# Other unread products in the norms, and new ones in front of gate and up pieces

## The chip, the core and the metric

The kernel runs on one core of a Trainium2 chip. The metric is the device time in microseconds (us) of one execution. Five engines share the core: TensorE (PE in the profile; its weight loads are PEld) multiplies, VectorE (DVE) and ScalarE (ACT) do elementwise work and copies, GpSimd (POOL) does nothing here after four fills, and SyncE (SP) issues the loads. Sixteen DMA engines move the data from HBM into the on-chip store (SBUF). PE writes its results into PSUM, in banks of 512 fp32 columns by 128 partitions.

## The reference

Four rows of 640 numbers go through attention, a gated MLP, the same attention and the same MLP again, in fp32 throughout:

```python
x = x + A(layernorm(x))      # q = x @ wq; softmax(q k / sqrt(128)) v per head; @ wo
x = x + B(layernorm(x))      # relu(x @ W_gate) * (x @ W_up) @ W_down
x = x + A(layernorm(x))
x = x + B(layernorm(x))
```

Attention has 32 heads of 128 and looks at the last 1024 of 4096 cached keys and values, for each of the 4 batch rows. Keys, values and `wq`/`wo` are used in both layers, and so are `W_gate`, `W_up` (640 x 1728) and `W_down` (1728 x 640). The layer norm has no weights.

## The kernel before

All large operands lie in HBM as rows by partition, in the order of their use: `heads` (queries' weights, keys, values and output weights of the groups of four heads), `kept` (the same for the last 5 heads, groups K0 with three and K1 with two, which stay on chip from layer 0 to layer 1) and `mlp`. They stream through one tile, `store`, of 50,624 fp32 columns. `plan` (L116 to L198) lists every load: which columns of which row go to which place. `load` (L203) issues from the front of that list on SyncE's queue for as long as the place of the next load is free, and `done` (L245) marks columns as free after the last product that reads them, and calls `load`. The tile framework then makes SyncE wait for that product. So the loads keep the order of the plan, and a load whose place is still being read holds back everything behind it. In most of the run the pieces have up to 16,320 columns (8 MB). In layer 0's MLP the kept groups hold most of the store, and gate, up and down weights pass in pieces of 640 to 1344 columns through what is left; layer 1's first pieces of `heads` (L173 to L189) then go to places that layer 0's MLP and layer 1's work on the kept groups free one by one.

The order of instructions is the order in which the program is written; nothing rearranges it. A layer is `attention(layer)` (L484) and `forward(layer)` (L532). `normalized` (L337) opens both: VectorE sums `y` (L342), ScalarE copies it (L343), PE turns the partition sums into means by products with a selecting matrix (`mean`, L330, products at L334), VectorE subtracts the mean (L346), ScalarE squares and sums (L348), PE transposes the centred rows (L352 and L354) and VectorE copies them out as `xT` (L356), the stationary operand of all that follows. `deviation` gives the scale. In `attention`, `query` makes q of one group from `xT` (products through `product`, L242, into banks `m`), `query_turned` (L401) transposes it, `scores` multiplies with keys into `ps` (layer 1's first group: into `pp`), `softmax`, `turned` (L430), `values` into `po` and `project` into `y` follow. In `forward`, `gate(j)` (L536) makes a slice of gate and up: `gate(3)` the smaller rest first, then 0, 1 and 2. Each has 5 row chunks c by 4 column groups g (3 groups for the rest), each a product of 256 moving columns (128 for the rest) with 32 stationary ones, four side by side in the array by `tile_position`. `gated`, `hidden` and `down` finish the MLP.

A product whose result nobody reads is called an unread product here. The kernel has two helpers for them: `busy(n)` (L314) makes n transposes of the 128 x 128 identity into `po`, `fill(n)` (L321) n products of the identity with itself. Both only act while `waits[0]` is set. `normalized` sets it, `forward` sets it to `layer == 0` after `gate(3)`, and `values` to `layer == 0` at a layer's last group. In the norm, `busy(2)` stands between the sum and the mean (L344), and `fill(1)` between the squares and the transposes (L349).

The names of profile rows: L242 is `product`, so weights of all kinds go by the tile they write; L318 is `busy`, L325 is `fill`, L211 is the issue of a load. One fp32 product shows as two MATMULs, a transpose as one.

Of the kernel before, what the change touches and what calls it, by code (L numbers as in the profile page):

```python
# [13 lines left out]
P = 128  # L14
# [81 lines left out]
def decode_kernel(ctx: ExitStack, tc: tile.TileContext, x, source, sel, out):  # L96
    nc = tc.nc
# [42 lines left out]
    def near(c, row="heads"):  # L140

        return max(x for x in ROWS[row][2] if x <= c)
# [22 lines left out]
    lo = 0  # L165
# [6 lines left out]
    lo = HELD  # L172
# [9 lines left out]
    for n in 4096, 6144, 9728:  # L182
        hi = near(lo + n)
        to = put(1, "heads", to, lo, hi)
        lo = hi
    hi = near(lo + 4608)
    to = put(1, "heads", to, lo, hi)
    lo, hi = hi, near(hi + STORE - to)
# [12 lines left out]
    held = {}  # L201
# [18 lines left out]
    def place(layer, row, lo):  # L220

        if row == "heads" and lo < HELD:
            return first_q, lo, HELD - lo
        most = KV
        if row == "kept" and layer:
            if AHEAD[0] <= lo < AHEAD[1]:
                return probs, QUARTER + lo - AHEAD[0], AHEAD[1] - lo
            if BACK[0] <= lo < BACK[1]:
                return store, HOME + lo - BACK[0], BACK[1] - lo
            most = min(x - lo for x in (AHEAD[0], BACK[0], FRONT) if x > lo)  # L230
        for first, m, p in held[key(layer, row)]:
            if first <= lo < first + m:
                return store, p + lo - first, min(first + m - lo, most)
        raise KeyError((layer, row, lo))

    def product(out, by, layer, row, lo, n, start, stop, rows=slice(0, P), **how):

        a = 0
        while a < n:
            t, p, m = place(layer, row, lo + a)  # L240
            z = min(n, a + m)
            nc.tensor.matmul(out[:, a:z], by, t[rows, p:p + z - a], start=start and not a, stop=stop and z == n, **how)  # L242
            a = z

    def done(layer, row, lo, n):  # L245

        if row == "kept" and layer == 0:
            return
        if row == "kept":
            for p in range(lo, lo + n):  # L250
                if BACK[0] <= p < BACK[1]:
                    live[HOME + p - BACK[0]] = False
                elif not (AHEAD[0] <= p < AHEAD[1] or HOME <= p < HOME + BACK[1] - BACK[0]):
                    live[p] = False
        else:
            for first, m, p in held[key(layer, row)]:
                a, b = max(lo, first) - first, min(lo + n, first + m) - first
                if a < b:
                    live[p + a:p + b] = [False] * (b - a)
        load()  # L260
# [12 lines left out]
    sel_sb = const.tile([P, P + 32], F32, name="sel_sb")  # L273
# [14 lines left out]
    pp = ps_p.tile([P, 2, 512], F32, name="pp")  # L288
# [6 lines left out]
    def bank(n):  # L295

        turn_of[0] ^= 1
        return banks[turn_of[0]][:, :n]
# [4 lines left out]
    ident, sel_q = sel_sb[:, :P], sel_sb[:, P:]  # L303
# [6 lines left out]
    for g in range(4):  # L310
        nc.tensor.matmul(y[32 * g:32 * g + B], ident[:B, :B], probs[:B, g * QUARTER:(g + 1) * QUARTER],
                         start=True, stop=True, tile_position=(0, 32 * g))

    def busy(n):  # L314

        if waits[0]:
            for _ in range(n):
                nc.tensor.transpose(po[:, :P], ident, ident)  # L318


    def fill(n, to=po):  # L321

        if waits[0]:
            for _ in range(n):
                nc.tensor.matmul(to[:, :P], ident, ident, start=True, stop=True)  # L325


    waits = [False]

    def mean(a):  # L330

        m = bank(1)
        for g in range(4):
            nc.tensor.matmul(m[32 * g:32 * g + 32], sel_q, a, start=True, stop=True, tile_position=(0, 32 * g))  # L334
        return m

    def normalized():  # L337

        ysb, xc, sq = probs[:, :QUARTER], gates[:, :QUARTER], gates[:, QUARTER:2 * QUARTER]
        waits[0] = True  # L340
        su = small.tile([P, 1], F32, name="su", bufs=1)
        nc.vector.tensor_reduce(su, y, axis=AX.X, op=ALU.add)  # L342
        nc.scalar.copy(ysb, y)  # L343
        busy(2)  # L344
        mu = mean(su)
        nc.vector.tensor_tensor(xc, ysb, mu.to_broadcast([P, QUARTER]), op=ALU.subtract)  # L346
        ss = small.tile([P, 1], F32, name="ss", bufs=1)
        nc.scalar.activation(sq, xc, AF.Square, accum_out=ss)  # L348
        fill(1)  # L349

        pt = pp[:, 0, :KC * 32].rearrange("p (c x) -> p c x", c=KC)
        nc.tensor.transpose(pt[:, :4], xc[:, :P], ident)  # L352
        for g in range(4):
            nc.tensor.matmul(pt[32 * g:32 * g + 32, 4, :B], xc[:, P:], ident[:, 32 * g:32 * g + B],  # L354
                             start=True, stop=True, tile_position=(0, 32 * g))
        nc.vector.tensor_copy(xT[:, :KC * B].rearrange("p (c b) -> p c b", b=B), pt[:, :, :B])  # L356
        return ss
# [13 lines left out]
    def go_on():  # L371

        nc.tensor.matmul(y, ident, probs[:, :QUARTER], start=True, stop=False)
# [157 lines left out]

    def forward(layer):  # L532
        ss = normalized()
        gus, hTs = {}, {}

        def gate(j):  # L536
            n, groups = (P, 4) if j < 3 else (64, 3)
            at = GU0 + j * GU if j < 3 else 0
            gus[j] = pp[:, j % 2, :2 * P]
            for c in range(KC):  # L540
                for g in range(groups):
                    lo = at + (c * groups + g) * 2 * n
                    product(gus[j][32 * g:32 * g + 32], xT[:, B * c:B * c + 32], layer, "mlp", lo, 2 * n,
                            start=c == 0, stop=c == KC - 1, tile_position=(0, 32 * g))
                    done(layer, "mlp", lo, 2 * n)

        def gated(j):
            n, p = (P, P) if j < 3 else (64, 96)
            gu = gus.pop(j)
            at = 256 * (j % 2)  # L550
            a, b = gates[:p, at:at + n], gates[:p, at + P:at + P + n]
            nc.scalar.activation(a, gu[:p, :n], AF.Relu, scale=rstd[:p])
            nc.vector.scalar_tensor_tensor(b, gu[:p, n:2 * n], rstd[:p], a, op0=ALU.mult, op1=ALU.mult)
            return b

        def hidden(j, h):
            hTs[j] = small.tile([P, 4, B], F32, name="hT", bufs=4)
            ph = bank(P).rearrange("p (f x) -> p f x", f=4)
            if j < 3:
                nc.tensor.transpose(ph, h, ident)  # L560
                nc.vector.tensor_copy(hTs[j], ph[:, :, :B])
                return

            for g, lo, f in (0, 0, 0), (1, 64, 0), (2, 0, 1), (2, 64, 1):
                nc.tensor.matmul(ph[lo:lo + 64, f, :B], h, ident[:96, 32 * g:32 * g + B],
                                 start=True, stop=True, tile_position=(0, lo))
            nc.vector.tensor_copy(hTs[j][:, :2], ph[:, :2, :B])

        def down(j, last=False):
            for f in range(4 if j < 3 else 1):  # L570
                lo = WD1 + j * WD + f * D if j < 3 else WD0
                for g in range(4):
                    product(y[32 * g:32 * g + B], hTs[j][:, f], layer, "mlp", lo + g * QUARTER, QUARTER,
                            start=False, stop=last and f == 3, tile_position=(0, 32 * g))
                done(layer, "mlp", lo, D)
                if j == 3:
                    fill(1)
                elif not (last and f > 1):
                    busy(1)
                if j == 0 and f == 1:  # L580
                    fill(2)
            if j == 3:
                for g in range(4):
                    r = slice(64 * (g // 2), 64 * (g // 2) + 64)
                    product(y[32 * g:32 * g + B], hTs[j][r, 1], layer, "mlp", TAIL + g % 2 * QUARTER, QUARTER,
                            start=False, stop=False, rows=r, tile_position=(r.start, 32 * g))
                done(layer, "mlp", TAIL, 2 * QUARTER)

        gate(3)
        waits[0] = layer == 0  # L590
        rstd = deviation(ss)
        go_on()
        fill(1)
        h = gated(3)
        for j, j1 in (3, 0), (0, 1), (1, 2):
            gate(j1)
            hidden(j, h)
            fill(1)
            h = gated(j1)
        down(3)  # L600
        down(0)
        hidden(2, h)
        if layer == 0:
            nc.scalar.copy(away[:, :512].rearrange("p (j n) -> p j n", j=2), pp[:, :, 256:])
            for i in range(2):
                nc.scalar.copy(away[:, 512 + 384 * i:896 + 384 * i], banks[i][:, P:])
            live[AWAY[0]:AWAY[1]] = [True] * 1280
        down(1)
        down(2, last=True)
# [64 lines left out]
```

## Time and profile before

| | |
|---|---|
| time, median of 3 runs | 731.74 us (731.72 to 732.07) |
| profiled execution, its own time | 734.14 us |
| its span, first to last instruction | 732.4 us |
| mean granted clock of PE | 0.816 |
| busy: PE, PEld, DVE, ACT | 445.4, 158.6, 75.2, 54.2 us |
| bytes read from HBM | 310.57 MB, mean 424 GB/s over the span |

The profiled execution has its own time, 734.14 us, beside the median of the unprofiled ones, and its span leaves out what lies before the first and after the last instruction. PE's busy time is the time in which at least one product is under way, not a measure of how much it does. The granted clock is the share of full speed that the chip gave PE. "DMA share" in a window is the mean over the 16 DMA engines of the time in which they have packets under way, and can come out slightly above 1 in short windows.

### The profile page before, as it was taken

What the parts mean: (1) busy time and instruction counts of PE and PEld (TensorE: products, weight loads), DVE (VectorE), ACT (ScalarE), POOL (GpSimd) and SP (SyncE); (2) the same over time, 40 slices, a digit from 0 to 9 for tenths busy, and PEclk for the clock granted to TensorE, in tenths of its full rate; (3) what the DMA queues carried; (4) which work ended last, traced back from release to release, by engine and by line L of the source; (5) the groups of instructions that cost most, each with busy time, mean ns of one, the idle gap of its engine ahead of it and who ended that gap; (6) DMA issues with size and microseconds to landing.
All of it is one profiled execution on the core that took longest, in us unless ns stands there. A gap on an engine that the chain in (4) does not pass through costs nothing.

```text
span 732.4 us, 8422 instructions
## 1 busy us (share of the span) xinstructions
PE 445.4 (61%) x3844; PEld 158.6 (22%) x3844; DVE 75.2 (10%) x279; ACT 54.2 (7%) x101; POOL 0.2 (0%) x4
## 2 busy tenths in 40 slices
PE   0845565655655554619879896365656555556576
PEld 0211112222112121103344241021121112112123
DVE  1111001010010101002101211001010010101011
ACT  0200000000000000001302210000000000000100
POOL 0000000000000000000000000000000000000000
PEclk9888887776777777759999999677787878778989
DMA  9999999999999999999999999999999999999996
GB/s 405 445 405 438 440 445 416 434 431 444 441 419 428 419 441 448 419 431 425 419 392 407 392 427 455 423 441 434 433 427 444 424 441 426 438 437 420 423 429 286
DMA packets 13291, 311.19 MB, mean 425 GB/s; under 512 B 1476, under 2 KB 1732, under 8 KB 6984
## 3 DMA queue, kind: packets, MB, share of 16 engines
q1 hardware_dynamic: 13104, 310.56, 98.9%
q8 instruction: 30, 0.49, 0.2%
q10 hardware_dynamic: 152, 0.09, 0.0%
q14 instruction: 5, 0.04, 0.0%
HBM read 310.57 MB, written 0.08 MB: 424 GB/s over the span
## 4 chain that ended last, share of the span: by engine, by line
DMA 73%; PE 22%; another core or an unknown queue 3%; DVE 1%; issue 1%; SPq 0%; ACT 0%; DVEq 0%; ACTq 0%
DMA store<-in_heads 57%; DMA store<-in_kept 9%; PE ps L242 9%; DMA store<-in_mlp 7%; PE po L242 6%; PE m L242 2%; PE pp L242 1%; PE y L242 1%; PE pp L430 1%; PE m L401 1%; PE m L470 0%; PE m L461 0%; DVE gates L394 0%; SPq L211 0%
## 5 line engine op out<-in xcount | busy, mean ns | idle before, releaser
L242 PE MATMUL po<-store,pT 128*16 128x512 f32 (+2 forms) x1044 | 155.4, 707 | 130.4 <-DMA store<-in_heads 125.0
L242 PE MATMUL ps<-store,qT 128*4 128x512 f32 (+3 forms) x1016 | 151.7, 682 | 109.9 <-DMA store<-in_heads 89.4
L242 PEld LDWEIGHTS po<-store,pT 128*16 128x16 f32 x1044 | 38.4, 110 | 234.3 <-DMA store<-in_heads 124.7
L242 PEld LDWEIGHTS ps<-store,qT 128*4 128x4 f32 x1016 | 36.3, 94 | 206.7 <-DMA store<-in_heads 99.9
L422 DVE TENSOR_REDUCE nm<-ps 128x1 f32<-128x1024 f32 x17 | 20.8, 1224 | 242.4 <-PE ps L242 242.4
L426 ACT ACTIVATE probs<-ps,nm 128x1024 f32<-128x1024 f32 x17 | 18.9, 1114 | 328.9 <-DVE nm L422 328.9
L242 PE MATMUL m<-store,xT 128*32 128x512 f32 (+5 forms) x152 | 30.3, 600 | 10.5 <-DMA store<-in_heads 10.5
L440 DVE COPY pT<-pp 128x16 f32<-128x16 f32 x128 | 17.1, 168 | 140.2 <-PE po L242 140.2
L457 ACT COPY gates<-po 128x512 f32<-128x512 f32 x16 | 9.4, 586 | 249.5 <-PE po L242 249.5
L242 PE MATMUL pp<-store,xT 128*32 128x256 f32 (+3 forms) x322 | 21.0, 371 | 7.4 <-DMA store<-in_mlp 3.5
L242 PE MATMUL y<-store,oT 128*4 128x160 f32 x512 | 23.3, 314 | 1.3 <-DVE oT L474 1.1
L430 PE MATMUL pp<-sel_sb,probs 128*128 128x128 f32 x144 | 20.4, 289 | 0.0
L430 PEld LDWEIGHTS pp<-sel_sb,probs 128*128 128x128 f32 x144 | 17.9, 150 | 0.0
L463 DVE RECIPROCAL r<-m 128x16 f32<-128x16 f32 x18 | 4.6, 258 | 129.1 <-PE m L461 129.1
L242 PEld LDWEIGHTS y<-store,oT 128*4 128x4 f32 x512 | 13.2, 90 | 9.3 <-issue 3.9
L394 DVE TENSOR_SCALAR gates<-m,rstd 128x512 f32<-128x512 f32 (+2 forms) x18 | 12.4, 690 | 26.6 <-PE m L242 26.6
L242 PEld LDWEIGHTS pp<-store,xT 128*32 128x32 f32 x322 | 11.3, 114 | 15.2 <-DMA store<-in_mlp 6.7
L401 PE MATMUL m<-sel_sb,gates 128*128 128x128 f32 x64 | 12.8, 325 | 0.0
L242 PE MATMUL y<-store,hT 128*4 128x160 f32 (+1 forms) x224 | 11.2, 299 | 2.4 <-DMA store<-in_mlp 2.2
L470 PE MATMUL m<-sel_sb,gates 128*128 128x128 f32 x72 | 12.0, 289 | 0.8 <-DVE gates L450 0.8
L401 PEld LDWEIGHTS m<-sel_sb,gates 128*128 128x128 f32 x64 | 7.9, 159 | 20.0 <-issue 20.0
L242 PEld LDWEIGHTS m<-store,xT 128*32 128x32 f32 x152 | 7.2, 124 | 22.3 <-DMA store<-in_heads 11.7
(80 smaller groups left out, 124.1 us busy)
## 6 DMA issues: line engine op xcount, KB each, us to landing
store<-in_heads SPq DMA_DIRECT2D x22, 8000.0 KB, 45.7
store<-in_heads SPq DMA_DIRECT2D x1, 7776.0 KB, 45.5
store<-in_heads SPq DMA_DIRECT2D x1, 7744.0 KB, 46.0
store<-in_heads SPq DMA_DIRECT2D x1, 7424.0 KB, 44.6
store<-in_heads SPq DMA_DIRECT2D x1, 7360.0 KB, 35.3
store<-in_heads SPq DMA_DIRECT2D x1, 7168.0 KB, 33.6
store<-in_mlp SPq DMA_DIRECT2D x10, 640.0 KB, 7.4
store<-in_heads SPq DMA_DIRECT2D x1, 6400.0 KB, 44.4
```

What stands on the lines that cost most here:

```text
L242: nc.tensor.matmul(out[:, a:z], by, t[rows, p:p + z - a], start=start and not a, stop=stop and z == n, **how)
L394: nc.vector.tensor_scalar(gates[:, :len(HEADS[g]) * P], qp.pop(g), rstd, SCALE, op0=ALU.mult, op1=ALU.mult)
L401: nc.tensor.transpose(qt[:, i], gates[:, i * P:(i + 1) * P], ident)
L422: nc.vector.tensor_reduce(nm[g], to.rearrange("p j n -> p (j n)"), axis=AX.X, op=ALU.max, negate=True)
L426: nc.scalar.activation(probs, sc.pop(g).rearrange("p j n -> p (j n)"), AF.Exp, bias=nm.pop(g), accum_out=sums[g])
L430: nc.tensor.transpose(pp[:, c // 4, c % 4 * P:c % 4 * P + P], probs[:, c * P:(c + 1) * P], ident)
L440: nc.vector.tensor_copy(to[:, 4 * j:4 * j + 4], pp[:, j].rearrange("p (c x) -> p c x", c=4)[:, :, i:P:32])
L457: nc.scalar.copy(gates, po)
L463: nc.vector.reciprocal(r[g], so.rearrange("p (b i) -> p i b", b=B)[:, :SIDE])
L470: nc.tensor.transpose(ot[:, 127 * b:127 * b + P], gates[:, b * P:(b + 1) * P], ident)
```

## The change

A new helper, `wide`, makes two unread products with 32 stationary columns (the first 32 of the identity) and 160 moving columns (`sel_sb`, which is the identity and 32 columns more) into the first 32 partitions of bank 1 of `pp`. It acts always. In `normalized` it takes the place of `busy(2)` and of `fill(1)`. In `gate`, one `fill` product is put in front of a product in whose columns a loaded piece of more than 900 columns begins, if it is in chunk 3 or 4 or in `gate(1)` or `gate(2)`; `fill` acts only while `waits[0]` is set. Loads, their places and all products that are read stay as they are.

```diff
+    def wide():
+        for _ in range(2):
+            nc.tensor.matmul(pp[:32, 1, :P + 32], ident[:, :32], sel_sb, start=True, stop=True)
...
         nc.vector.tensor_reduce(su, y, axis=AX.X, op=ALU.add)
         nc.scalar.copy(ysb, y)
-        busy(2)
+        wide()
         mu = mean(su)
         nc.vector.tensor_tensor(xc, ysb, mu.to_broadcast([P, QUARTER]), op=ALU.subtract)
         ss = small.tile([P, 1], F32, name="ss", bufs=1)
         nc.scalar.activation(sq, xc, AF.Square, accum_out=ss)
-        fill(1)
+        wide()
...
             for c in range(KC):
                 for g in range(groups):
                     lo = at + (c * groups + g) * 2 * n
+                    if c > 2 or j in (1, 2):
+                        fill(any(lo <= first < lo + 2 * n and m > 900 for first, m, _ in held[layer, "mlp"]))
                     product(gus[j][32 * g:32 * g + 32], xT[:, B * c:B * c + 32], layer, "mlp", lo, 2 * n,
                             start=c == 0, stop=c == KC - 1, tile_position=(0, 32 * g))
```

## The prediction

> **What bounds the kernel now.** I read the page's busy shares and chain of waits first, then windows of the stretches in which the chain leaves the large loads, then the timeline there.
>
> ```profile
> span 732.4 us, 8422 instructions
> DMA 73%; PE 22%; another core or an unknown queue 3%; DVE 1%; issue 1%; SPq 0%; ACT 0%; DVEq 0%; ACTq 0%
> q1 hardware_dynamic: 13104, 310.56, 98.9%
> ```
>
> 73% of the chain is loads, and the one load queue has packets under way in 98.9% of the 16 engines' time. TensorE (PE) is no bound as a whole. It matters only where it frees the store too late for the next load. Windows over the run (the columns at the end are granted clock, DMA share, GB/s) find that place:
>
> ```profile
> 12.00:360.00 348.00, 200.38 (x1541) 67.85 (x1543) 32.67 (x120) 22.89 (x38) 0.00 (x0) 0.79 1.00 432
> 360.00:402.00 42.00, 35.37 (x461) 17.92 (x457) 5.30 (x20) 8.51 (x22) 0.00 (x0) 0.92 1.01 402
> 402.00:409.00 7.00, 6.97 (x63) 2.21 (x63) 1.27 (x3) 1.72 (x3) 0.00 (x0) 1.00 0.92 306
> 409.00:722.00 313.00, 197.25 (x1675) 68.11 (x1670) 32.85 (x125) 19.43 (x36) 0.00 (x0) 0.81 1.00 433
> ```
>
> Before 360 and after 409 us the loads run at 432 and 433 GB/s whatever PE does, even at a mean clock of 0.79. At 402 to 409 us, the start of layer 1, they run at 306: against 433 that loses 7 x (433 - 306)/433 = 2.05 us. The share there is still 0.92, so on average an engine is empty for only 7 x 0.08 = 0.56 us; the rest is packets that take longer.
>
> Why the loads run thin there: the granted clock falls twice, each time for one window of 3.41 us, and the second drop lies on layer 1's first query projections.
>
> ```profile
> 371.34:374.75 3.41, 2.04 (x26) 0.99 (x20) 0.42 (x2) 0.37 (x1) 0.00 (x0) 1.00 0.99 376
> 374.75:378.16 3.41, 3.34 (x35) 2.05 (x37) 0.00 (x0) 0.00 (x0) 0.00 (x0) 0.50 1.02 384
> 381.58:384.99 3.41, 1.71 (x31) 0.97 (x27) 0.00 (x0) 0.00 (x0) 0.00 (x0) 1.00 0.96 383
> 395.23:398.64 3.41, 2.90 (x52) 1.49 (x48) 0.82 (x3) 0.77 (x4) 0.00 (x0) 1.00 0.96 377
> 398.64:402.06 3.42, 3.42 (x26) 1.26 (x26) 0.78 (x2) 1.70 (x3) 0.00 (x0) 0.50 1.02 408
> ```
>
> Busy time does not decide the drop: PE was busy 2.90 us before the second one, and only 1.71 us in a window that is followed by full clock. What was streamed does. The groups of PE in the three windows that end at 374.75 (dropped), 384.99 (kept) and 398.64 (dropped), in this order:
>
> ```profile
> L242 PE MATMUL pp<-store,xT 128*32 128x256 f32 x16 | 1.7, 389 | 1.3 <-DMA store<-in_mlp 1.3
> L325 PE MATMUL po<-sel_sb 128*128 128x128 f32 x2 | 0.5, 326 | 0.0
> ...
> L242 PE MATMUL pp<-store,xT 128*32 128x256 f32 x21 | 2.2, 387 | 0.0
> L242 PE MATMUL pp<-store,xT 128*32 128x128 f32 x10 | 2.0, 280 | 1.7 <-DMA store<-in_mlp 1.7
> ...
> L242 PE MATMUL y<-store,hT 128*4 128x160 f32 x20 | 1.2, 299 | 0.2 <-DMA store<-in_mlp 0.2
> L318 PE MATMUL po<-sel_sb 128*128 128x128 f32 x3 | 0.8, 309 | 0.0
> L325 PE MATMUL po<-sel_sb 128*128 128x128 f32 x2 | 0.5, 326 | 0.0
> L352 PE MATMUL pp<-sel_sb,gates 128*128 128x128 f32 x1 | 0.3, 328 | 0.1
> ```
>
> Products at four places (those of L242) run four at once, so I count their columns over four. Moving columns: 4 x 256 + 2 x 128 = 1280, dropped; 21/4 x 256 + 10/4 x 128 = 1664, kept; 5 x 160 + 6 x 128 = 1568, dropped. The number of stationary columns is not in this count: the kept window had 32 of them throughout. An estimate from these rows: full clock needs some 1600 moving columns in the window before.
>
> **The change, part by part.** A column's price comes from eight transposes of 128 columns at full and at half clock, in the chain of waits, where the queries and the end stand too:
>
> ```profile
> 1.64 45.70 DMA store<-in_heads
> ...
> 181.59 1.71 PE pp L430 x8
> ...
> 398.63 3.52 PE m L242 x26
> ...
> 411.65 0.87 PE pp L430 x8
> ...
> 698.16 30.63 DMA store<-in_mlp
> ```
>
> 0.87/(8 x 128) = 0.85 ns a column at full clock, 1.67 at half.
>
> *Norms.* A `fill` product is two MATMULs (L325 x2 above), a `busy` transpose one. Each norm drops 2 + 2 MATMULs of 128 columns and gets two places of 4 MATMULs of 160: a place grows from 256 to 640 columns, from 0.22 to 0.54 us, without a DMA. They write bank 1 of `pp`, whose last readers ended well before each norm. Layer 1's attention norm:
>
> ```profile
> 396.47 0.44 PE L318 MATMUL po<-sel_sb 128*128 128x128 f32 x2
> 396.61 0.32 DVE L342 TENSOR_REDUCE su<-y 128x1 f32<-128x160 f32 x1 [5.14 <-PE y L242]
> 397.08 0.24 PE L334 MATMUL m<-su,sel_sb 128*32 128x1 f32 x8 [0.17 <-DVE su L342]
> 397.25 0.49 PE L325 MATMUL po<-sel_sb 128*128 128x128 f32 x2
> 397.45 0.32 DVE L346 TENSOR_TENSOR gates<-probs,m 128x160 f32<-128x160 f32 x1 [0.52 <-PE m L334]
> 397.83 0.33 PE L352 MATMUL pp<-sel_sb,gates 128*128 128x128 f32 x1
> ```
>
> The first place streams from 396.47 to 397.01 and the product behind it (L334) waits for the sum until 397.08; the second from 397.25 to 397.79, against 397.83. VectorE's two steps of 0.32 us are the cover; without it each place costs its growth, 0.32 us. Queued behind on PE are the norm's own products, then the queries that free the store. Bounds for one norm 0 to 0.64; I take 0.1, since cover and stream differ by under 0.1. Two norms lie where PE frees space (365 and 396 us): 0 to +1.28, taken +0.2 on PE. The run's first norm is covered by the 45.70 us of loads that open the chain, the last (708 us) by the 30.63 us of loads that end the run: 0 each, 0.64 if PE were last there.
>
> *In front of pieces.* The condition gives seven products, all in layer 0: one in `gate(0)`, three each in `gate(1)` and `gate(2)`; in layer 1 `waits` is off by then. Each streams 256 columns, 0.22 us. PE's idle time before four of these places:
>
> ```profile
> 372.85 1.05 PE L242 MATMUL pp<-store,xT 128*32 128x256 f32 x10 [1.27 <-DMA store<-in_mlp]
> 378.86 0.64 PE L242 MATMUL pp<-store,xT 128*32 128x64 f32 x10 [0.27 <-DMA store<-in_mlp]
> 382.95 0.84 PE L242 MATMUL pp<-store,xT 128*32 128x128 f32 x12 [0.70 <-DMA store<-in_mlp]
> 384.79 1.54 PE L242 MATMUL pp<-store,xT 128*32 128x128 f32 x18 [1.00 <-DMA store<-in_mlp]
> ```
>
> All four waits are longer than 0.22 us: nothing. The other three cost 0 to 0.22 each, so 0 to +0.66 in all; taken +0.1. Without this cover all seven would cost 1.5.
>
> *Clock at 398.64.* The window before it goes from 1568 to 1568 - 512 + 1280 = 2336 columns, well past the kept 1664, so I expect full clock. The queries' 3.52 us become 1.76. What waits for them:
>
> ```profile
> SPq L211 <- PE m L242: 4.9, 2, 3.6
> ```
>
> SyncE's load queue stands 4.9 us behind these queries and everything behind comes as late; it moves up by at most 1.76 us, which bounds the gain: 0 to -1.76. How much reaches the end? The 16 engines do not finish together:
>
> ```profile
> 725.00:725.50 0.50, 0.00 (x0) 0.00 (x0) 0.17 (x1) 0.00 (x0) 0.00 (x0) 1.00 0.81 328
> 727.50:728.00 0.50, 0.50 (x16) 0.22 (x8) 0.00 (x0) 0.00 (x0) 0.00 (x0) 1.00 0.24 97
> 728.00:728.50 0.50, 0.49 (x12) 0.11 (x8) 0.00 (x0) 0.00 (x0) 0.00 (x0) 1.00 0.08 31
> ```
>
> The share falls from 0.81 to 0.08 over 3 us, and 0.08 of 16 is about one engine. The run ends with the engine that is furthest behind, and such an engine still has packets when the others run dry at 403 to 407. Filling that hole mostly lets the leaders lead by more. I take half of the average engine's idle time, 0.56/2, about -0.3.
>
> *Clock at 374.75.* The fill in `gate(0)` lifts that window from 1280 to 1536: between my two dropped counts and the kept one, undecided. If the clock stays full, the rate of 376 and 384 could rise to the stretch's 402: at most 6.83 x (402 - 380)/402 = 0.37 us. Taken at -0.1. [...]
>
> *Sum.* PE's +0.2 and +0.1 reach the end only through the same thin loads, a third of them: +0.1. With -0.3 and -0.1 that is -0.3: the profiled execution's 734.14 us (span 732.4) becomes 733.8. It stands 2.40 above the median of the runs, 731.74, so I expect **731.4** there.
>
> **Rivals.**
> 1. *The whole hole is filled.* The engine that ends last does run dry at 402 to 409, so the queue's earlier start counts in full: -1.76 - 0.37 + 0.1 = -2.0, 729.7. For it: 306 GB/s is far below 433. Against: the share of 0.92 and the staggered end.
> 2. *The clock does not change*, because 32 stationary columns count less, or because the timed executions have no drop there: only the costs stay, +0.1, 731.8. For it: 1568 and 1664 lie so close that a window shifted by one product decides, and the runs agree within 0.35 us. [...]
> 3. *Slower: the unread products outlast the waits they stand in.* Place: the two middle norms and the seven pieces; price 1.28 + 1.5 = +2.8, 734.5. It decides once VectorE's sum is ready more than 0.1 us before the 0.54 us are streamed, or a piece has landed before its fill starts. Against: the six rows of the norm and the four waits.
>
> **How the numbers follow.** Forecast 0.50, rival 1 0.15, rival 2 0.27, rival 3 0.08. A measurement here tells about 0.2%, 1.46 us, from no change. Faster by more: rival 1 and a little of the forecast, 0.17; slower by more: most of rival 3, 0.07; within: 0.76. The range goes down most of the way to rival 1 and up to a part of rival 3: 730.0 to 732.4.
>
> **What would show it.** Right: clock 1.00 in the 3.4 us after layer 1's attention norm, the 26 query products in about 1.8 us, SyncE's wait for them about halved, over 350 GB/s at 402 to 409, and yet an end that moves by half a microsecond or less. Wrong: clock 0.50 there (rival 2); an end earlier by nearly as much as the queue (rival 1); L334 or L352 over 0.2 us later after their sums than now, or idle time in front of the seven pieces gone while the loads thin out (rival 3).

## The result and the profile after

The changed kernel takes 733.96 us (median of 20 runs, 732.25 to 735.41), the kernel before 731.82 us (20 runs beside them); the ratio is 1.0026 (95%: 1.0019 to 1.0033). It is slower, and outside the range of 730.0 to 732.4.

One thing has to be known for all that follows. The profiled execution of before on which the prediction was made took 734.14 us, 2.40 above the median, and was one of that kernel's rare slower ones: 20 of the 166 executions of before that were timed beside the kernels of this document took over 733 us (one of 1275.45 us left out). The usual one is read here from a second trace of the same unchanged kernel, whose own time was 732.43. "Before" below means that second trace. The 20 executions of the changed kernel fall into ten from 732.25 to 733.61 and ten from 734.31 to 735.41; its trace, with its own time of 734.39, is one of the upper ten.

The page of after, then its windows (the last three columns are granted clock, DMA share, GB/s):

```profile
span 732.6 us, 8482 instructions
DMA 72%; PE 23%; another core or an unknown queue 3%; issue 1%; DVE 1%; SPq 0%; ACT 0%; DVEq 0%; ACTq 0%
```

```profile
12.00:360.00 348.00, 198.82 (x1544) 67.40 (x1546) 32.66 (x120) 22.89 (x38) 0.00 (x0) 0.79 1.00 432
360.00:402.00 42.00, 37.51 (x485) 20.17 (x480) 4.82 (x20) 8.01 (x21) 0.00 (x0) 0.96 1.00 391
402.00:409.00 7.00, 6.97 (x66) 2.15 (x63) 1.26 (x4) 2.23 (x5) 0.00 (x0) 1.00 0.98 379
409.00:722.00 313.00, 196.95 (x1683) 69.12 (x1675) 33.32 (x125) 19.63 (x37) 0.00 (x0) 0.81 1.00 433
376.00:384.00 8.00, 7.38 (x80) 4.46 (x75) 0.49 (x2) 0.37 (x1) 0.00 (x0) 1.00 1.00 380
396.00:402.00 6.00, 5.88 (x87) 2.95 (x84) 1.13 (x5) 1.97 (x5) 0.00 (x0) 0.79 0.93 329
391.67:395.08 3.41, 2.01 (x29) 0.76 (x28) 0.00 (x0) 0.52 (x2) 0.00 (x0) 1.00 1.04 410
395.08:398.49 3.41, 3.41 (x35) 1.23 (x36) 0.00 (x0) 0.00 (x0) 0.00 (x0) 0.50 0.98 375
```

The windows of before, second trace:

```profile
360.00:402.00 42.00, 35.07 (x482) 17.50 (x480) 5.88 (x22) 8.50 (x22) 0.00 (x0) 1.00 1.01 402
402.00:409.00 7.00, 6.38 (x55) 1.54 (x44) 1.81 (x3) 2.93 (x5) 0.00 (x0) 1.00 1.03 420
376.00:384.00 8.00, 5.14 (x65) 2.46 (x65) 0.49 (x2) 0.37 (x1) 0.00 (x0) 1.00 1.02 407
396.00:402.00 6.00, 5.61 (x80) 2.85 (x76) 2.20 (x7) 2.47 (x6) 0.00 (x0) 1.00 0.99 381
```

The shares of the chain stay and the long stretches run at 432 and 433 GB/s as before. What is lost lies in 376 to 384 (380 GB/s against 407), around which six of the seven unread products lie (375.15 to 384.29), in 396 to 402 (329 against 381), where after's clock is halved, and in 402 to 409 (379 against 420): by these rates some 0.5, 0.8 and 0.7 us. This execution of before has no clock drop from 360 to 412 us and hardly a hole: there was little to be won. After has a drop of its own at 395.08, some 3.6 us earlier than the first trace's second one.

The timeline of PE in after, `gate(1)` and `gate(2)` (start, duration, group, idle time before):

```profile
374.59 0.63 PE L242 MATMUL pp<-store,xT 128*32 128x256 f32 x4
375.15 0.49 PE L325 MATMUL po<-sel_sb 128*128 128x128 f32 x2
375.57 1.05 PE L242 MATMUL pp<-store,xT 128*32 128x128 f32 x12
376.55 0.49 PE L325 MATMUL po<-sel_sb 128*128 128x128 f32 x2
376.97 1.26 PE L242 MATMUL pp<-store,xT 128*32 128x128 f32 x20
378.16 0.49 PE L325 MATMUL po<-sel_sb 128*128 128x128 f32 x2
...
393.97 0.46 PE L242 MATMUL y<-store,hT 128*4 128x160 f32 x8 [1.40 <-DMA store<-in_mlp]
```

The same of before:

```profile
374.61 1.25 PE L242 MATMUL pp<-store,xT 128*32 128x256 f32 x18
376.69 1.57 PE L242 MATMUL pp<-store,xT 128*32 128x128 f32 x20 [0.83 <-DMA store<-in_mlp]
...
392.60 0.46 PE L242 MATMUL y<-store,hT 128*4 128x160 f32 x8 [0.16 <-DMA store<-in_mlp]
```

Before ran 18 MATMULs and then waited 0.83 us. In after an unread product stands in front of number 5 and of number 17: the second one stands ahead of two MATMULs that in before ran without a wait. The place explains it, and run 4 below tests that. A piece of a load ends in the middle of a product, so `product` (L242) splits it: its first part reads the last columns of the piece before, and with that its space is free; only its second part waits for the new piece. `fill` stands in front of the whole, so of the part that frees the store. And a place takes more than it streams, as the chain of waits of after shows (start, duration):

```profile
381.55 0.42 PE po L325 x2
381.97 0.98 PE pp L242 x6
382.95 0.42 PE po L325 x2
...
385.81 8.12 DMA store<-in_mlp
393.97 0.46 PE y L242 x8
...
400.77 1.86 PE m L242 x26
```

0.42 us, not 0.22. And the pieces' products around it take longer too: in before 18 of them take 1.25 us; in after the first 16 take 0.56 (374.59 to 375.15) and 0.98 us (375.57 to 376.55), and the last two some 0.4, until the load goes out at 377.41. That is 0.7 us more, beside the 0.84 of the two unread products. What this holds back shows in SyncE's timeline, the issues of loads, after first and then before:

```profile
377.41 0.33 SPq L211 DMA_DIRECT2D store<-in_mlp  x1
383.74 0.33 SPq L211 DMA_DIRECT2D store<-in_mlp  x1
395.13 0.33 SPq L211 DMA_DIRECT2D store<-in_heads  x1
398.74 0.33 SPq L211 DMA_DIRECT2D store<-in_heads  x1
```

```profile
375.90 0.33 SPq L211 DMA_DIRECT2D store<-in_mlp  x1
382.20 0.33 SPq L211 DMA_DIRECT2D store<-in_mlp  x1
393.76 0.97 SPq L211 DMA_DIRECT2D store<-in_heads  x2
396.31 0.33 SPq L211 DMA_DIRECT2D store<-in_heads  x1
```

The load in `gate(1)` goes out 1.51 us later, the one in `gate(2)` 1.54, each behind two places: some 0.76 us a place. The loads run thinner, the `mlp` piece that `down` needs arrives late, PE waits 1.40 us for it at 393.97 instead of 0.16 at 392.60, and what it frees then comes 1.37 us late (395.13). Behind this wait the clock is halved for one window, and the load that before issued at 396.31 goes out 2.43 us late (398.74). The span is 2.0 us longer.

### The profile page after: what moved, and what is told of

It reads as the page before. It is cut to its first block, busy times and chain, and to the rows that moved or that the text cites. A ratio compares the mean times of both kernels' runs of the same rounds, so it can differ in the third digit from the quotient of the medians.

```text
span 732.6 us, 8482 instructions
## 1 busy us (share of the span) xinstructions
PE 445.4 (61%) x3874; PEld 161.3 (22%) x3874; DVE 75.2 (10%) x279; ACT 54.2 (7%) x101; POOL 0.2 (0%) x4
## 4 chain that ended last, share of the span: by engine, by line
DMA 72%; PE 23%; another core or an unknown queue 3%; issue 1%; DVE 1%; SPq 0%; ACT 0%; DVEq 0%; ACTq 0%
DMA store<-in_heads 57%; DMA store<-in_kept 9%; PE ps L242 9%; DMA store<-in_mlp 6%; PE po L242 6%; PE m L242 2%; PE pp L242 2%; PE y L242 1%; PE pp L436 1%; PE m L407 1%; PE m L476 0%; PE m L467 0%; PE pp L331 0%; SPq L211 0%
## 5 line engine op out<-in xcount | busy, mean ns | idle before, releaser
L242 PE MATMUL po<-store,pT 128*16 128x512 f32 (+2 forms) x1044 | 155.3, 705 | 130.1 <-DMA store<-in_heads 124.6
L242 PE MATMUL ps<-store,qT 128*4 128x512 f32 (+3 forms) x1016 | 148.1, 668 | 114.1 <-DMA store<-in_heads 93.4
L242 PEld LDWEIGHTS po<-store,pT 128*16 128x16 f32 x1044 | 38.2, 110 | 233.6 <-DMA store<-in_heads 124.2
L242 PEld LDWEIGHTS ps<-store,qT 128*4 128x4 f32 x1016 | 36.0, 93 | 208.6 <-DMA store<-in_heads 103.9
L242 PE MATMUL m<-store,xT 128*32 128x512 f32 (+5 forms) x152 | 27.5, 553 | 8.8 <-DMA store<-in_heads 8.8
L242 PE MATMUL pp<-store,xT 128*32 128x256 f32 (+3 forms) x322 | 20.8, 349 | 4.4 <-DVE gates L561 3.0
L242 PE MATMUL y<-store,oT 128*4 128x160 f32 x512 | 22.6, 311 | 1.3 <-DVE oT L480 1.1
L242 PEld LDWEIGHTS y<-store,oT 128*4 128x4 f32 x512 | 13.0, 89 | 9.2 <-issue 3.9
L242 PE MATMUL y<-store,hT 128*4 128x160 f32 (+1 forms) x224 | 12.0, 320 | 4.1 <-DMA store<-in_mlp 3.8
L242 PEld LDWEIGHTS pp<-store,xT 128*32 128x32 f32 x322 | 11.3, 109 | 9.8 <-DVE gates L561 4.2
```

## The experiments

Kernels in one group ran on the same chip. GB/s, the issues of the two loads (those at 375.90 and 382.20 in before) and the clock come from each kernel's trace; "clock halved" is said of 360 to 412 us.

| kernel | median us | before, same chip | ratio (95%) | GB/s 376–384 | load in `gate(1)`, `gate(2)` | GB/s 402–409 | clock halved |
|---|---|---|---|---|---|---|---|
| change, first time | 733.96 | 731.82 | 1.0026 (1.0019–1.0033) | 380 | 377.41, 383.74 | 379 | yes |
| 1 before again | 732.40 | 732.01 | 1.0003 (0.9994–1.0012) | 407 | 375.90, 382.20 | 420 | no |
| 2 norms only | 731.91 | 732.01 | 0.9997 (0.9988–1.0006) | 404 | 375.83, 382.05 | 418 | no |
| 3 pieces only | 734.75 | 732.01 | 1.0031 (1.0019–1.0043) | 377 | 377.75, 384.00 | 317 | yes |
| 4 before the waiting part | 732.14 | 732.11 | 0.9996 (0.9987–1.0004) | 406 | 376.49, 382.82 | 412 | no |
| 5 one column tile | 732.05 | 732.11 | 0.9996 (0.9987–1.0005) | 403 | 376.17, 382.38 | 410 | no |
| 6 `gate(1)` only | 732.73 | 732.11 | 1.0004 (0.9995–1.0013) | 374 | 377.24, 381.99 | 354 | yes |
| 7 `gate(2)` only | 732.43 | 732.11 | 1.0003 (0.9992–1.0013) | 398 | 375.96, 383.74 | 375 | no |
| 8 four tiles | 731.94 | 731.97 | 0.9994 (0.9985–1.0004) | 410 | 376.14, 382.44 | 421 | no |
| 9 quiet norm | 733.59 | 731.97 | 1.0014 (1.0002–1.0026) | 411 | 375.73, 382.03 | 321 | yes |
| 10 doubled | 733.28 | 731.97 | 1.0015 (1.0004–1.0027) | 370 | 377.78, 384.18 | 410 | no |
| 11 norms again | 731.97 | 731.97 | 0.9998 (0.9989–1.0008) | 405 | 375.83, 382.12 | 426 | no |
| 12 `down` tiled | 733.44 | 732.23 | 1.0010 (1.0001–1.0019) | 378 | 377.35, 383.60 | 353 | no |
| 13 change again | 733.27 | 732.23 | 1.0012 (1.0004–1.0021) | 387 | 377.30, 383.61 | 335 | yes |
| 14 all tiled | 732.24 | 732.23 | 0.9997 (0.9988–1.0005) | 408 | 376.08, 382.42 | 418 | no |
| 15 four tiles twice | 732.00 | 732.04 | 0.9999 (0.9990–1.0008) | 405 | 376.91, 383.23 | 407 | no |
| 16 change, third time | 733.69 | 732.04 | 1.0023 (1.0014–1.0032) | 380 | 377.49, 383.77 | 346 | yes |

The traces' own times fall into groups by the last columns. Eight traces without a clock drop and with both loads at most 1.0 us late (runs 1, 2, 4, 5, 8, 11, 14 and 15) took 731.66 to 732.62 us; the three without a drop in which one or both loads are 1.4 us late or more (7, 10, 12) 732.85 to 733.46; and the six with a drop 733.57 to 735.43: run 9, without a late load, 733.57, and 6, 13, 16, the change and 3, with late ones, 733.77, 733.88, 734.29, 734.39 and 735.43. (The first trace of before, with two drops, took 734.14.)

**Which part (1 to 3).** Before unchanged; the change without the products at the pieces; those alone (norms as before):

```diff
-                    if c > 2 or j in (1, 2):
-                        fill(any(lo <= first < lo + 2 * n and m > 900 for first, m, _ in held[layer, "mlp"]))
```

```diff
-        wide()
+        busy(2)
...
-        wide()
+        fill(1)
```

> The kernel before, unchanged, as a control and for a second trace of it. If its trace is typical of its runs: a span near 730.0, the time 731.8, and either a half clock at layer 1's start or none, according to where the 3.41 us windows fall. If the trace before was slowed by being taken: a span near 732.4 again beside runs at 731.8. Ratio 1.000 in either case.

> The norms' new unread products alone, none in front of pieces. Theory A (the products in front of pieces cost the time): 731.6 to 732.0, as before. Theory B (the longer places in the norms cost it): 733.5 to 734.0. Theory C (each part delays PE in the same short loop of loads, and the delays add): about 732.5.

> The unread products in front of gate and up pieces alone, norms as before. Theory A (these cost the time): 733.5 to 734.0. Theory B (the norms cost it): 731.6 to 732.0. Theory C (the delays add): about 733.3.

The norms alone cost and bring nothing; the pieces alone are slower by at least as much as the change (734.75, above the 733.5 to 734.0 expected). Run 11 repeated the norms (its expectation stands with runs 9 and 12 below): nothing again. One of its 11 executions took 733.12 us, so whether the longer places prevent the rare slower executions stays open.

**Place or kind (4 and 5).** The fill moved between the two parts, in front of the one that waits (`product` calls it, `ahead` is true where the condition was); and, at the old place, one product of 32 stationary columns in the column tile of the product behind it:

```diff
+            if ahead:
+                fill(any(first == lo + a and m > 900 for first, m, _ in held[layer, row]))
```

```diff
-    fill(any(lo <= first < lo + 2 * n and m > 900 for first, m, _ in held[layer, "mlp"]))
+    if waits[0] and any(lo <= first < lo + 2 * n and m > 900 for first, m, _ in held[layer, "mlp"]):
+        nc.tensor.matmul(po[32 * g:32 * g + 32, :P], ident[:, :32], ident, start=True, stop=True,
+                         tile_position=(0, 32 * g))
```

> The change with the seven unread products each moved by at most one part: six of the seven products in front of which they stand are split in two where the new piece begins, the first part reads the piece before and frees it, and only the second part waits for the new piece. Here the unread product stands in front of the second part. Theory P (the place costs: they delay the part that frees the piece before, so the next load is issued late): 731.7 to 732.5, as with the norms alone. Theory Q (PE time costs, wherever the seven stand): 733.5 to 734.5, as the change. Theory R (they do nothing; the clock drops at layer 1's start decide): scattered as the change, 732.3 to 735.5.

> The change with the seven unread products on 32 stationary columns in the same column tile as the product behind them, in place of the whole array, at the places of the change. A full one takes 0.42 us of PE's order in the trace and not 0.22, since the four column tiles run empty before and after it. Theory S (this emptying is most of the price): 731.9 to 732.8. Theory P (any product in front of the freeing part delays it): 732.8 to 733.6, about half the price. Theory Q with a price by streamed columns: 733.5 to 734.5.

Each takes the loss away: the loads in `gate(1)` and `gate(2)` go out 0.2 to 0.6 us later than before instead of 1.5, and 376 to 384 keeps 406 and 403 GB/s.

**How many (6, 7, 10).** The condition cut to `gate(1)`, in the same way to `gate(2)`, and two products at each of the seven places:

```diff
-                    if c > 2 or j in (1, 2):
+                    if j == 1:
```

```diff
-    fill(any(lo <= first < lo + 2 * n and m > 900 for first, m, _ in held[layer, "mlp"]))
+    fill(2 * any(lo <= first < lo + 2 * n and m > 900 for first, m, _ in held[layer, "mlp"]))
```

> The change with unread products in front of gate(1)'s three pieces only. In the traces the load issued at 375.90 us in the kernel before comes at 377.41 with the change, the first large delay. Theory P: most of the loss is here, 733.0 to 734.0. Theory Q (PE time): three sevenths of 2.1 us, 732.8.

> The change with unread products in front of gate(2)'s three pieces only. Theory P: here too a first part stands behind each of the three, so 732.5 to 733.5; if the first delay in gate(1) is what matters, 731.8 to 732.3. Theory Q: three sevenths of 2.1 us, 732.8.

> The change with two unread whole-array products in place of one at each of the seven places. If the lateness of the freeing parts is the cause: the delay at each place grows from about 0.65 to 0.87 us or more, the time by another 1 to 2.5 us, 735 to 736.5. If it is a matter of the single emptying of the tiles alone: 734.0 to 734.5. If the clock is what matters, twice the columns keep it up: 732 to 733.5.

Halves can't be told from before by their times. The 732.73 of `gate(1)` alone is below theory P's 733.0 to 734.0 and near theory Q's 732.8, but the intervals decide nothing. In the traces each makes its own load late (377.24; 383.74) and leaves the other, and 376 to 384 is thin with the first late (374), hardly with the second (398). In run 6 PE then waits 1.55 us for a piece in `gate(2)`, and the halved clock is there, from 383.43 to 386.84, not at layer 1's start. Doubling shows the price of a place in its chain of waits:

```profile
381.54 0.64 PE po L325 x4
382.18 0.99 PE pp L242 x6
```

0.64 for two products and 0.42 for one: 0.22 us of streaming each, and 0.20 once for a place. The loads are later still (377.78, 384.18; 0.2 us more for each place) and 376 to 384 thinner (370), but the 735 to 736.5 expected did not come: the time is not above the change's. In its trace, one of the faster executions (732.85), PE waits for no `down` piece as long as in after, the clock doesn't drop and 402 to 409 runs at 410 GB/s. Why is not explained.

**Emptying or streaming (8 and 15).** Four products, one in each column tile, at each place, and eight:

```diff
-    fill(any(lo <= first < lo + 2 * n and m > 900 for first, m, _ in held[layer, "mlp"]))
+    if waits[0] and any(lo <= first < lo + 2 * n and m > 900 for first, m, _ in held[layer, "mlp"]):
+        for k in range(4):
+            nc.tensor.matmul(po[32 * k:32 * k + 32, :P], ident[:, :32], ident, start=True, stop=True,
+                             tile_position=(0, 32 * k))
```

```diff
-        for k in range(4):
+        for k in 2 * [0, 1, 2, 3]:
```

> The change with each of the seven unread products replaced by four of 32 stationary columns, one in each column tile: the same columns streamed through the whole array, but without leaving the four column tiles. Theory S (running the four tiles empty before and after a whole-array product is most of the price): 731.9 to 732.8. Theory T (the array's time in front of the freeing part is the price, 0.22 us each): 733.3 to 734.2.

> The change with each of the seven unread whole-array products in front of a piece replaced by eight products of 32 stationary columns, two in each of the four column tiles. By its own streaming a place then takes twice 0.22 us, as long as the 0.42 us that a whole-array product takes in PE's order (0.64 us for two, so 0.42 is 0.22 of streaming and 0.20 of emptying the column tiles). Theory A, it is the time in PE's order ahead of the part that frees the store, however it comes about: as slow as the change, 1.2 us over the kernel before, loads at about 380 GB/s from 376 to 384 us. Theory B, it is the emptying of the column tiles, and products that share the array with the pieces can slip into the waits of single tiles: within 0.4 us of the kernel before, about 405 GB/s from 376 to 384 us.

> The changed kernel as it is, on the chip of the kernel with eight column-tile products at each place: 1 to 2 us over the kernel before. If the loss is set by what the loads show from 376 to 384 us, 380 to 393 GB/s there against 396 to 420 for kernels as fast as before; if only a dropped clock makes it, a trace without a drop shows the time of before.

Four cost nothing, and eight, which stream 0.44 us at a place, neither; the change on the chip of the eight costs 1.65. Four hold back the two loads by 0.24 us, eight by 1.0, the change by 1.5, and with eight 376 to 384 stays full:

```profile
376.00:384.00 8.00, 7.33 (x151) 5.46 (x143) 0.49 (x2) 0.37 (x1) 0.00 (x0) 1.00 1.02 405
```

So the streamed columns are not the price. Four tile products stream the same columns as one whole-array product, 0.22 us, and make a load 0.12 us late a place, not 0.76; eight take as long by their streaming as a whole-array product does in PE's order (0.44 and 0.42 us) and make it 0.5 late. What a whole-array product costs beyond its streaming, some 0.5 us a place, goes with leaving the four column tiles: 0.20 shows in its own 0.42 us, the rest in the pieces' products around it. With eight tile products at a place the loads are thus 1.0 us late, which cost nothing, with the change 1.4 us or more, which did: of the traces in the table, those with the first load at 376.91 or earlier and the second at 383.23 or earlier run at 403 to 411 in 376 to 384, those with both at 377.30 and 383.60 or later at 370 to 387. Why the limit lies between 1.0 and 1.4 us no run shows. PE's timelines of `gate(2)`, after first and then run 15 (L552 are its unread products), show the column tiles empty around a whole-array product:

```profile
381.48 0.49 PE L325 MATMUL po<-sel_sb 128*128 128x128 f32 x2
381.90 1.05 PE L242 MATMUL pp<-store,xT 128*32 128x128 f32 x12
382.88 0.49 PE L325 MATMUL po<-sel_sb 128*128 128x128 f32 x2
383.30 1.05 PE L242 MATMUL pp<-store,xT 128*32 128x128 f32 x12
```

```profile
381.45 0.50 PE L552 MATMUL po<-sel_sb 128*32 128x128 f32 x10
381.70 0.41 PE L242 MATMUL pp<-store,xT 128*32 128x128 f32 x2
381.77 0.28 PE L552 MATMUL po<-sel_sb 128*32 128x128 f32 x2
381.81 0.71 PE L242 MATMUL pp<-store,xT 128*32 128x128 f32 x9
```

In after each row overlaps the next by only 0.07 us; in run 15 the unread row of 381.77 lies wholly within the pieces' row of 381.70.

**Lateness and the clock (9, 12, 13).** Run 9 is before without the two transposes and the product in layer 1's attention norm; only unread products are left out. Run 12 is the change with `down`'s unread transposes in layer 0 replaced by four column-tile products each, made by `tiled` as in run 8, beside the change again.

```diff
-        busy(2)
+        busy(0 if quiet else 2)
...
-        fill(1)
+        fill(0 if quiet else 1)
...
-        rstd = deviation(normalized())
+        rstd = deviation(normalized(layer == 1))
```

```diff
-                    busy(1)
+                    tiled(1)
```

> The kernel before without the unread products in the norm of layer 1's attention (two transposes and one product left out), so that the window before layer 1's first queries holds 512 moving columns fewer and the clock should drop there in most executions instead of rarely. As in the prediction (the hole in the loads hardly reaches the end): 732.0 to 732.4, no cluster above. Rival 1 (the queries' lateness reaches the end in full): most executions at 733.5 to 734.5, the others near 732.0. If nothing drops: as before, 732.0.

> The norms' new unread products alone once more, for the rare slow executions: 11 of 84 executions of the kernel before so far were above 733 us, none of 11 with the longer places in the norms. If those are executions in which the clock drops at layer 1's start, and the longer places prevent it: median 731.8 to 732.1 and none above 733. If they have another cause: one or two above 733.

> The change, and in layer 0's down products each unread transpose replaced by four unread products, one in each column tile (256 columns in place of 128, and no emptying of the tiles), so that the windows before layer 1's first queries hold more columns. If the clock drop makes the upper cluster of the change: its late loads stay (377.4 and 383.7 us), but no drop between 391 and 402 us, and 732.3 to 733.3, none above 734. If the lateness alone costs the 2.1 us: 733.5 to 734.5 as the change.

> The change unchanged, on the same chip as the other two. 733.5 to 734.3, ratio 1.002 to 1.003, executions in two groups. If its trace is in the lower group, it has no half clock between 391 and 402 us; if in the upper group, it has one.

Run 9 makes a drop without any late piece, on layer 1's queries as in the first trace of before:

```profile
394.84:398.25 3.41, 2.10 (x46) 0.98 (x50) 0.82 (x3) 0.82 (x4) 0.00 (x0) 1.00 1.01 387
398.25:401.66 3.41, 3.41 (x27) 1.27 (x27) 0.78 (x2) 1.65 (x3) 0.00 (x0) 0.50 1.04 418
```

Its times are two at 731.68 and 731.89 and nine from 733.29 to 734.79: the drop's hole reaches the end with some 1.6 us (medians 733.59 and 731.97). Run 12 is the other half, lateness with no drop. PE's timeline, its groups in the clock's window with the wait, 392.58 to 395.99, and SyncE's timeline:

```profile
393.57 0.46 PE L242 MATMUL y<-store,hT 128*4 128x160 f32 x8 [1.23 <-DMA store<-in_mlp]
```

```profile
L242 PE MATMUL y<-store,hT 128*4 128x160 f32 x36 | 2.1, 299 | 1.3 <-DMA store<-in_mlp 1.2
L339 PE MATMUL po<-sel_sb 128*32 128x128 f32 x32 | 1.6, 273 | 0.0
```

```profile
394.58 0.82 SPq L211 DMA_DIRECT2D store<-in_heads  x2
400.29 0.33 SPq L211 DMA_DIRECT2D store<-in_heads  x1
```

The pieces are as late as in the change and PE waits 1.23 us for the `down` piece, at full clock throughout. The load behind goes out at 394.58 against 393.76, and a later one at 400.29 against 399.42 in before: 0.8 to 0.9 us late, and it stays so; 402 to 409 runs at 353 and the span is 0.8 longer (731.4 against 730.6). So lateness costs without the clock; runs 7 and 10, without a drop too, have spans of 731.7 and 731.1. In after's trace the lateness grows by 2.43 - 1.37 = 1.06 us over the window with half the clock. Yet run 12 is not faster than the change beside it (733.44, 733.27), three of its 12 executions are above 734 where none was expected, and run 13 itself is below the 733.5 to 734.3 expected: how often each kernel has the drop, and so how the change's 1 to 2 us divide, stays open.

**A better version (14).** Norms as in the change, `wide`, with four column-tile products both at the pieces and in `down`:

```diff
-    fill(any(lo <= first < lo + 2 * n and m > 900 for first, m, _ in held[layer, "mlp"]))
+    tiled(any(lo <= first < lo + 2 * n and m > 900 for first, m, _ in held[layer, "mlp"]))
...
-                    busy(1)
+                    tiled(1)
```

> The norms as in the change, and the unread products in front of pieces and among layer 0's down products all as four products in the column tiles: no late freeing, no drop. If emptying the tiles among the down products costs nothing now: 731.6 to 732.0, as with the norms alone. If it holds back loads there too: 731.0 to 731.5, faster than both kernels.

Its time is that of before. No version here beats the kernel before.

## Why the prediction was wrong

- **The bound: right.** Loads set the end, and only where PE frees the store late is time lost. The windows of the traces show it: 432 and 433 GB/s in the long stretches of both kernels, 380 against 407 in 376 to 384, where the change makes the loads late.
- **The trace it started from: wrong to build on.** The sum took -0.3 and -0.1 from two clock drops, though the execution stood 2.40 us above the median of runs that agree within 0.35. Rival 2 named it ("the timed executions have no drop there") and had the chance of 0.27. The second trace shows full clock in all of 360 to 402 and 420 GB/s behind, so the 0.4 us that the sum takes off had nothing to come from in such an execution. So two executions of the same kernel, one with the drop and one without, are both on record. Nor do the windows lie at one place in every execution. Within the first trace the clock's changes lie whole multiples of 3.41 us apart (the two drops 7, the full clock from 402.06 to 456.67 us 16 times). Counted from the first instruction, the second drop begins at 398.64 us there, run 9's at 398.25 and run 6's at 383.43: 0.39 and 15.21 us earlier, no multiples of it.
- **Half of the engine's idle time: a wrong step, that no longer mattered.** "Filling that hole mostly lets the leaders lead by more" took 0.28 of 2.05 us. Run 9 makes such a hole (321 GB/s) and loses 1.6 us: rival 1's pricing, nearly the whole.
- **Some 1600 moving columns for full clock: not a threshold.** The groups of PE in after's window 391.67 to 395.08, which is followed by 0.50, and in run 3's window 372.40 to 375.82, which is followed by 1.00:

```profile
L242 PE MATMUL y<-store,hT 128*4 128x160 f32 x25 | 1.7, 299 | 1.4 <-DMA store<-in_mlp 1.4
L318 PE MATMUL po<-sel_sb 128*128 128x128 f32 x4 | 1.4, 356 | 0.0
...
L242 PE MATMUL pp<-store,xT 128*32 128x256 f32 x14 | 1.7, 389 | 1.1 <-DMA store<-in_mlp 1.0
L325 PE MATMUL po<-sel_sb 128*128 128x128 f32 x4 | 1.0, 326 | 0.0
```

  25/4 x 160 + 4 x 128 = 1512, dropped; 14/4 x 256 + 4 x 128 = 1408, kept. In runs 13 and 16 the windows before the drop count 1632. Run 12's groups above make 36/4 x 160 + 32/4 x 128 = 2464, kept. So many more columns (2464) kept the clock, but between 1408 and 1632 the count doesn't decide, and what does stays open. That the norm's unread products bear on the clock behind them is read from run 9, where they are left out: the clock behind is halved (0.50 from 398.25 to 401.66), and 9 of its 11 executions took over 733 us, against 20 of 166 of before. The queries ran at full clock in 1.86 us in after, as forecast, but so they do in before's second trace (1.86), so that is no proof of the wider places. The drop had moved to a window that the forecast had not looked at, the one with the wait of 1.40 us.
- **Norms, +0.2: right to within what can be told.** Runs 2 and 11 are at -0.10 and 0.00 us.
- **In front of pieces, "All four waits are longer than 0.22 us: nothing": the step that failed.** This term of the sum was taken at +0.1 us, and the pieces alone cost 2.7 by the medians (run 3). It failed twice. The price is 0.42 us in PE's order and some 0.76 at the load; the quoted row of a `fill` says 0.49 us for its two MATMULs, but it was priced by its streamed columns alone. And the rows with idle time were taken for the places: the fill stands in front of the whole product, two MATMULs earlier than the wait, so it isn't covered by that wait but holds back the part that frees the store, and with it a load, by 1.5 us. Moving it by those two (run 4) makes "nothing" true.
- **Rival 3: the right side, with another mechanism.** It was right that the kernel gets slower and that the pieces do it. The norms that it counted too cost nothing, and it decided by whether "a piece has landed before its fill starts". What decides is whether the fill is in front of an instruction that frees a place, and whether the load for it is then more than 1.0 us late (1.4 and more cost). The loss was 1.0 to 2.1 us (733.27 to 732.23, 733.96 to 731.82), not 2.8.

## What to carry to other kernels

Idle time ahead of a row covers an unread product only if the product is issued right in front of the instruction that waits; look which instruction ahead of the wait frees a buffer, and put nothing in front of that one (in front of the part that waits the seven products made the two loads 0.6 us late, in front of the part that frees 1.5). Between products that share the array by column tiles, use unread products in the same tiles: they made a load 0.12 us late a place here, a whole-array one 0.76. Compare a profile's own time with the median of the runs before a step of the sum rests on it, and take a second trace where they differ.

## What was not expected of the hardware

- A whole-array product between column-tiled ones took 0.42 us of PE's order, a second one behind it 0.22. With what the column-tiled products around it lost, it made a load 0.76 us late; the same columns in the four tiles 0.12.
- Loads that were issued 1.0 us late cost nothing (405 GB/s, 732.00 us), 1.4 to 1.5 us late (run 12) 0.8 us of span in a trace without any clock drop there (378 GB/s).
- Behind a window of 3.41 us with a wait of 1.40 us the clock was halved for one window, and the loads came another 1.06 us late. With four tile products in place of each transpose (run 12) a wait of 1.23 us was followed by full clock.
